# A causal softmax convolution and a cosine feed-forward layer on one core: weight conversion through PSUM scratch, row transposes from the third block on, and the last half block pair by pair

## The chip, the cores and the metric

The kernel runs on one core of a Trainium2 chip. The metric is device microseconds (us) of one execution. Before the change three runs gave 2300.47 us (median), 2298.91 and 2300.74. Engines are named as in the profile: PE (TensorE), PEld (its weight loads), DVE (VectorE), ACT (ScalarE), POOL (GpSimd), SP (the engine that issues all DMAs).

## The reference

```python
w = exp(weight_gen - max(weight_gen, -1)); w = w / (sum(w, -1) + 1e-9)   # (8, 4096, 8 heads, 7 taps)
x_pad = six zero rows ahead of x, along the sequence                      # x: (8, 4096, 192)
out[b, s, h, g] = sum over k of w[b, s, h, k] * x_pad[b, s + k, h, g]     # 8 heads of 24 columns
h = out.reshape(32768, 192) @ w_in                                        # w_in:  (192, 2048)
g = h * cos(h)
y = g @ w_out                                                             # w_out: (2048, 192)
```

The weights w_in and w_out arrive as 64-bit floats, everything else as 32-bit. The kernel splits each float operand of a product into a high part (fp32r) and a low part, and adds up the products of parts.

## The kernel before

**Blocks and periods.** Each of the 128 partitions holds 256 neighbouring rows of the sequence. A block is R = 4 of these rows on all partitions, 512 tokens; there are NB = 64 blocks. For each block POOL mixes the seven taps (`attention`: seven products, L239, and six additions, L256, in 128x768 tiles; its 13 steps are handed out two to four a period through `attentions`). PE turns the mixed block around (`transpose_all`, L292, into an `h` tile), and ACT and DVE split it (`split`, L282 and L284). The 2048 columns of h are taken in 8 pairs of 128-column chunks. A period i = 0..511 is one pair of one block: `ffn_in_first` and `ffn_in_second` (L322, L339) make h in PSUM; ACT rounds it to whole turns (L349), DVE takes the fraction (L353), ACT the sine (L357), DVE multiplies (L360), ACT makes the high part of g (L367) and DVE the low part (L371, called lo below). LAG = 6 periods later `ffn_out(j)` (L401) multiplies half a block of g, four pairs, by w_out, for two token rows at a time; `evacuate` copies the sums (L424, L428), and POOL adds the two halves (L441, L442). The last block does this on DVE.

**Two ways to transpose.** Blocks up to WHOLE = 6 go whole: in pair TR = 5 of the block before, eight PE transposes into an `h` tile, which ACT then copies out (L602). Later blocks go row by row (`transpose_row`, L301), into unused columns of the `acc` tile of `ffn_out`. They start at j = 8(b-2), that is at period 8b-10, whereas a whole transpose stands at period 8b-3. `until_mixed` makes sure that POOL's steps for the block have been issued ahead of it.

**PSUM.** `ps_h` has three tiles of 128x2x512 floats, `ps_m` one. An `h` tile is taken by the matmuls of a period and is free after its lo.

**Weights.** `two_parts` turns 64-bit words into 32-bit floats by integer operations: absolute value on ACT (L116), four DVE operations (L118, L121, L126, L130), casts on ACT (L132, L134), and the low part on POOL (L136). Its scratch `t1` lies in SBUF. Four pieces are converted before the first period or behind it, the other eleven in periods 1 to 9, by the table `late` (period of the conversion, loader, arguments), with their loads two periods ahead.

**Order.** Each engine executes in the order in which the Python code issues. SP carries the DMAs and, between them, small events (`traded`, L268) on which the second half of a period's matmuls waits. In period i the code issues for ACT and DVE: turns of i-1, high part of i-2, fraction of i-1, sine of i-1, conversion, lo of i-2, product of i-1; then the matmuls of i, loads, and the next steps of softmax and mixing. The prologue (L496 to L536) mixes block 0 on two engines, rows 0 to 2 on DVE and row 3 on POOL.

## Time and profile before

| | us |
|---|---|
| median of three runs | 2300.47 |
| the profiled execution | 2300.27 |
| its span, first to last instruction | 2298.4 |
| PE busy, of the span | 2215.7 (96%) |
| POOL busy | 2001.4 (87%) |
| DVE busy | 1935.6 (84%) |
| ACT busy | 1897.3 (83%) |
| first matmul of period 0 | 32.15 |
| first matmul of period 10 | 113.00 |
| last matmul ends, by its row | 2292.29 |

The rows in the prediction are of four kinds. The page's groups give a line, an engine, an operation, tiles and the count, then busy time and the mean ns of one. A row of the timeline gives the start in us, the duration, the engine and line, the tiles, the count of merged instructions, and in brackets the idle time before it with what ended it. A row of the windows gives for a stretch its length and each engine's busy time, then the granted PE clock, the DMA share and GB/s. A row of the chain gives start, length and the work merged into it.

### The profile page before, as it was taken

What the parts mean: (1) busy time and instruction counts of PE and PEld (TensorE: products, weight loads), DVE (VectorE), ACT (ScalarE), POOL (GpSimd) and SP (SyncE); (2) the same over time, 40 slices, a digit from 0 to 9 for tenths busy, and PEclk for the clock granted to TensorE, in tenths of its full rate; (3) what the DMA queues carried; (4) which work ended last, traced back from release to release, by engine and by line L of the source; (5) the groups of instructions that cost most, each with busy time, mean ns of one, the idle gap of its engine ahead of it and who ended that gap; (6) DMA issues with size and microseconds to landing.
All of it is one profiled execution on the core that took longest, in us unless ns stands there. A gap on an engine that the chain in (4) does not pass through costs nothing.

```text
span 2298.4 us, 60540 instructions
## 1 busy us (share of the span) xinstructions
PE 2215.7 (96%) x26472; PEld 2001.3 (87%) x26472; DVE 1935.6 (84%) x1664; ACT 1897.3 (83%) x2123; POOL 2001.4 (87%) x1445
## 2 busy tenths in 40 slices
PE   2699999999999999999999999999999999999998
PEld 1488888889899999998989888899998889999887
DVE  8988888888888888888888888888888888888886
ACT  2678888888888888888888888888888888888885
POOL 7679999899899989989899899989989899899940
PEclk9799999999999999999999999999999999999999
DMA  6112112112212112112212212212212212212100
GB/s 147 46 42 58 34 49 50 40 44 49 51 33 58 43 32 58 43 41 50 46 38 50 54 29 57 50 26 58 50 34 49 58 26 49 58 27 50 33 9 22
DMA packets 25767, 105.55 MB, mean 46 GB/s; under 512 B 2734, under 2 KB 6566, under 8 KB 25502
## 3 DMA queue, kind: packets, MB, share of 16 engines
q1 hardware_dynamic: 25502, 101.67, 18.5%
q8 instruction: 208, 3.41, 0.6%
q14 instruction: 57, 0.47, 0.1%
HBM read 76.50 MB, written 25.17 MB: 44 GB/s over the span
## 4 chain that ended last, share of the span: by engine, by line
PE 65%; POOL 19%; ACT 7%; DVE 6%; issue 3%; DMA 0%; SPq 0%; POOLq 0%; ACTq 0%
PE acc L401 31%; PE h L339 22%; PE h L322 11%; POOL xa L256 6%; POOL pr L239 6%; POOL part L441 2%; ACT part L424 2%; ACT turn L349 2%; POOL x_lo L284 1%; DVE glo L371 1%; ACT ghi L367 1%; POOL fin L442 1%; DVE turn L353 1%; ACT turn L357 1%; POOL taps L192 1%
## 5 line engine op out<-in xcount | busy, mean ns | idle before, releaser
L353 DVE TENSOR_TENSOR turn<-h,turn 128x1024 f32<-128x1024 f32 x512 | 625.7, 1222 | 277.4 <-ACT turn L349 277.4
L401 PE MATMUL acc<-wo,ghi 64*128 64x384 f32 x8144 | 815.4, 336 | 7.6 <-ACT part L428 3.9
L401 PEld LDWEIGHTS acc<-wo,ghi 64*128 64x128 f32 x8144 | 740.6, 185 | 49.1 <-ACT part L424 12.6
L256 POOL TENSOR_TENSOR xa<-xa,pr 128x768 f32<-128x768 f32 (+1 forms) x384 | 709.1, 1847 | 0.6
L357 ACT ACTIVATE turn<-turn 128x1024 f32<-128x1024 f32 x512 | 543.8, 1062 | 183.1 <-DVE turn L353 179.7
L360 DVE SCALAR_TENSOR_TENSOR h<-h,turn 128x1024 f32<-128x1024 f32 x512 | 631.0, 1232 | 49.4 <-ACT turn L357 49.3
L349 ACT ACTIVATE turn<-h 128x1024 int32<-128x1024 f32 x512 | 525.3, 1026 | 127.9 <-PE h L339 125.9
L371 DVE TENSOR_TENSOR glo<-h,ghi 128x1024 bf16<-128x1024 f32 x512 | 622.4, 1216 | 9.3 <-ACT ghi L367 9.3
L239 POOL TENSOR_TENSOR pr<-xt,taps 128x768 f32<-128x768 f32 (+1 forms) x384 | 592.2, 1543 | 12.2
L367 ACT CAST ghi<-h 128x1024 fp32r<-128x1024 f32 x512 | 518.1, 1012 | 17.8 <-DVE h L360 17.6
L401 PE MATMUL acc<-wo_b,glo 64*128 64x192 bf16 x8144 | 433.2, 243 | 0.0
L441 POOL TENSOR_TENSOR part<-part,part 128x768 f32<-128x768 f32 x126 | 233.0, 1850 | 174.5 <-ACT part L424 133.5
L401 PEld LDWEIGHTS <-glo 64*128 64x128 bf16 x8144 | 333.5, 94 | 27.6 <-issue 13.4
L339 PE MATMUL h<-x_lo,wa_hi 64*128 64x512 f32 x1024 | 252.4, 478 | 1.0
L322 PE MATMUL h<-x_lo,wa_hi 64*128 64x512 f32 x1024 | 216.8, 409 | 37.3 <-DVE glo L371 23.3
L424 ACT COPY part<-acc 128x1024 f32<-128x1024 f32 x228 | 227.0, 996 | 0.0
L339 PE MATMUL h<-x_lo,wb_hi 64*128 64x512 f32 x1024 | 210.7, 397 | 0.0
L339 PE MATMUL h<-x_hi,wa_hi 64*128 64x512 f32 x1024 | 210.6, 397 | 0.0
L322 PE MATMUL h<-x_hi,wa_lo 64*128 64x512 f32 x1024 | 209.1, 393 | 0.9 <-POOL wa_lo L136 0.8
L322 PE MATMUL h<-x_hi,wa_hi 64*128 64x512 f32 x1024 | 209.5, 394 | 0.0
L339 PE MATMUL h<-x_hi,wb_hi 64*128 64x512 f32 x1024 | 207.9, 391 | 0.0
L339 PE MATMUL h<-x_hi,wb_lo 64*128 64x512 f32 x1024 | 207.7, 391 | 0.0
(68 smaller groups left out, 2145.3 us busy)
## 6 DMA issues: line engine op xcount, KB each, us to landing
xt<-in_x_dram SPq DMA_DIRECT2D x62, 960.0 KB, 7.0
out_dram<-fin SPq DMA_DIRECT2D x63, 384.0 KB, 3.4
taps<-in_weight_gen_dram SPq DMA_DIRECT2D x15, 448.0 KB, 4.9
raw<-in_moe_w_out_dram SPq DMA_DIRECT2D x8, 384.0 KB, 3.4
raw<-in_moe_w_in_dram SPq DMA_DIRECT2D x10, 256.0 KB, 4.3
xt<-in_x_dram SPq DMA_DIRECT2D x1, 768.0 KB, 10.9
xt<-in_x_dram SPq DMA_DIRECT2D x1, 540.0 KB, 6.7
raw<-in_moe_w_in_dram SPq DMA_DIRECT2D x4, 128.0 KB, 5.8
```

The source lines that it names most:

```text
L239: eng.tensor_tensor(out=dst.rearrange("p r (h g) -> p r h g", h=H), in0=xt[:, k + ra:k + rb, :].rearrange("p r (h g) -> p r h g", h=H), in ...
L256: eng.tensor_tensor(out=xa[:, ra:rb], in0=xa[:, ra:rb], in1=old[:, ra:rb], op=ALU.add)
L322: nc.tensor.matmul(h[:, q, :], lhsT=w[rs, chunk(pair, q)], rhs=v[rs, q, :], start=(m == 0), stop=False, skip_group_check=True)
L339: nc.tensor.matmul(h[:, 1 - q, :], lhsT=w[rs, cs], rhs=v[rs, q ^ middle, :], start=False, stop=(m == len(prods) - 1), skip_group_check=True)
L349: nc.scalar.activation(out=t.bitcast(I32), in_=hs[i], func=AF.Identity, bias=0.25, scale=1.0)
L353: nc.vector.tensor_tensor(out=t, in0=hs[i], in1=t.bitcast(I32), op=ALU.subtract)
L357: nc.scalar.activation(out=t, in_=t, func=AF.Sin, bias=SIN_BIAS, scale=SIN_SCALE)
L360: nc.vector.scalar_tensor_tensor(out=hs[i], in0=hs[i], scalar=TWO_PI, in1=turns.pop(i), op0=ALU.mult, op1=ALU.mult)
L367: nc.scalar.copy(out=hi, in_=hs[i])
L371: nc.vector.tensor_tensor(out=lo, in0=hs.pop(i), in1=hi.bitcast(F32), op=ALU.subtract)
L401: nc.tensor.matmul(to, lhsT=g[rs, n, t * P:(t + 1) * P], rhs=w[rs, fc, :], start=(lo == 0 and c == 0 and (whole or s == 0)), stop=(lo == 1 ...
L441: eng.tensor_tensor(out=part, in0=part, in1=old, op=ALU.add)
```

## The change

- `two_parts` has a scratch of two halves handed to it by `make_room`: its sizes lie in an `h` tile of PSUM, only its last result in SBUF. The scale of the absolute value replaces one DVE operation, so three are left (L132, L136, L140 of the new file).
- In a period with a conversion the period's own `h` tile is taken first (`h_now`), then the scratch. Lo of i-2 now stands ahead of the conversion, the product of i-1 in its middle (after the casts of the conversion before, behind the sine).
- The prologue keeps block 0's sum for rows 0 to 2 and their taps in an `h` tile (`own`). Input rows are loaded ahead of weights, and the first weights are converted after the mixing. Three pieces of w_in (columns 0 to 255, a 512-wide piece for the `wb` table, columns 256 to 767) are converted there; before there were four.
- `late` gets a column for when to load; some loads use the tiles `part1` and `fin`, not yet needed then.
- WHOLE goes from 6 to 2: blocks 3 to 6 are transposed row by row. Mixing gets three steps a period up to period 11; the end of the softmax for blocks 3 to 6 moves from periods 10 to 12 to periods 6 to 8.
- The last four periods of `ffn_out` become `last_half`: all four token rows of the last half block, pair by pair, into two `h` tiles.

```diff
-    WHOLE = 6
+    WHOLE = 2
...
+    def make_room():
+        sizes = ps_h.tile([P, 2, CT], F32, name="h")
+        bits = work.tile([P, 2, CW], F32, name="t1", tag="turn", bufs=TMP)
+        room[:] = [(sizes[:, n, 0:CW].bitcast(I32), bits[:, n, :].bitcast(I32)) for n in range(2)]
...
-        t1 = work.tile([P, 2, CW], F32, name="t1", tag="turn", bufs=TMP)
-        size, bits = (shaped(t1.bitcast(I32)[:, k, 0:n])[..., 0] for k in range(2))
-        nc.scalar.activation(out=size.bitcast(F32), in_=top.bitcast(F32), func=AF.Abs)
+        size, bits = (shaped(t[:, 0:n], 1)[..., 0] for t in room.pop(0))
+        nc.scalar.activation(out=size.bitcast(F32), in_=top.bitcast(F32), func=AF.Abs, scale=F64_SCALE)
         yield
         nc.vector.tensor_scalar(
-            out=size.bitcast(F32), in0=size.bitcast(F32), scalar1=F64_SMALL, scalar2=None, op0=ALU.max)
-        yield
-        nc.vector.tensor_scalar(
-            out=size, in0=size, scalar1=0x07FFFFFF, scalar2=3,
-            op0=ALU.bitwise_and, op1=ALU.logical_shift_left)
+            out=size, in0=size, scalar1=3, scalar2=None, op0=ALU.logical_shift_left)
...
+    def last_half():
+
+        b = NB - 1
+        tiles = [ps_h.tile([P, 2, CT], F32, name="h") for _ in range(2)]
+        for p in range(HALF):
+            for lo in range(2):
+                g = g_parts[b * NPAIR + HALF + p][lo]
+                for t in range(R):
+                    acc = tiles[t // 2][:, t % 2, 0:(D if lo else 2 * D)]
+                    for n in range(2):
+                        fc = 2 * (HALF + p) + n
+                        nc.tensor.matmul(
+                            acc, lhsT=g[:, n, t * P:(t + 1) * P], rhs=(wo_b if lo else wo)[:, fc, :],
+                            start=(p == 0 and lo == 0 and n == 0),
+                            stop=(p == HALF - 1 and lo == 1 and n == 1), skip_group_check=True)
+        fin = work.tile([P, R, D], F32, name="fin")
+        for t in range(R):
+            old = sums.pop((b, t // 2))[:, t % 2] if t % 2 else sums[(b, t // 2)][:, 0]
+            part_ = work.tile([P, 2, CT], F32, name="part1", bufs=2)
+            part = part_[:, 0, 0:2 * D]
+            nc.vector.tensor_tensor(out=part, in0=tiles[t // 2][:, t % 2, 0:2 * D], in1=old, op=ALU.add)
+            (nc.vector if t == R - 1 else nc.gpsimd).tensor_tensor(
+                out=fin[:, t, :], in0=part[:, 0:D], in1=part[:, D:2 * D], op=ALU.add)
...
+    own = ps_h.tile([P, 2, CT], F32, name="h")
+    sm0 = softmax(0, R, nc.vector, to=own_taps)
     next(sm0)
-    b0 = w_in_b(0)
-    a0 = w_in_a(0, 256)
     load_rows(0)
     sm1 = softmax(R, 3 * R, nc.gpsimd)
     next(sm1)
-    a1 = w_in_a(256, 512)
-    b1 = w_in_b(1)
+    w_a0 = w_in_a(0, 256)
+    w_b0 = w_in_b(0)
     load_rows(1)
+    w_a1 = w_in_a(256, 768)
...
+        converts_now = converts.get(i, ())
+        h_now = None
+        if converts_now:
+            h_now = ps_h.tile([P, 2, CT], F32, name="h")
...
-        for c in converts.get(i - 1, ()):
-            next(c)
         if 0 <= i - 1 < N:
             dve_fraction(i - 1)
             act_cos(i - 1)
+        if 0 <= i - 2 < N:
+            dve_lo(i - 2)
+        if converts_now:
+            make_room()
+        for c in converts_now:
+            next(c)
+        all_of(*converts.pop(i - 1, ()))
         for c in now:
             next(c)
         splits.extend(later)
-        all_of(*converts.pop(i - 1, ()))
-        if 0 <= i - 2 < N:
-            dve_lo(i - 2)
         if 0 <= i - 1 < N:
             dve_g(i - 1)
+        for _ in range(3):
+            for c in converts_now:
+                next(c)
         all_of(*now)
```

How the instructions move is seen on two engines. First DVE, in a period that converts two pieces of w_out (`t` with a number is the SBUF scratch, `h` a PSUM tile, `raw` the loaded words). Before, from the fraction of period 1 on:

```order
L353 TENSOR_TENSOR turn<-h,turn 128x1024
L118 TENSOR_SCALAR t_307<-t_307 128x384
L118 TENSOR_SCALAR t_309<-t_309 128x384
L121 TENSOR_SCALAR t_307<-t_307 128x384
L121 TENSOR_SCALAR t_309<-t_309 128x384
L126 SCALAR_TENSOR_TENSOR t_307<-raw,t_307 128x384
L126 SCALAR_TENSOR_TENSOR t_309<-raw,t_309 128x384
L130 SCALAR_TENSOR_TENSOR t_307<-raw,t_307 128x384
L130 SCALAR_TENSOR_TENSOR t_309<-raw,t_309 128x384
L371 TENSOR_TENSOR glo<-h,ghi 128x1024
L360 SCALAR_TENSOR_TENSOR h<-h,turn 128x1024
```

And with the change, from the fraction of period 3 on:

```order
L369 TENSOR_TENSOR turn<-h,turn 128x1024
L387 TENSOR_TENSOR glo<-h,ghi 128x1024
L376 SCALAR_TENSOR_TENSOR h<-h,turn 128x1024
L132 TENSOR_SCALAR h<-h 128x384 x2
L136 SCALAR_TENSOR_TENSOR h<-raw,h 128x384 x2
L140 SCALAR_TENSOR_TENSOR t_402<-raw,h 128x384 x2
```

Lo and the product have moved ahead of the conversion, two of eight conversion operations are gone, and none of the six that are left has two inputs in SBUF. Of the three `h` tiles one is the scratch while such periods last; the order's waits show that period i's first matmul then waits for lo of period i-2, where it waited for lo of i-3.

Second PE, at the end of the program (`acc` is the tile of `ffn_out`, `ghi` with a number is the high part of one pair; rows of weight loads and of the low parts are left out). Before, the last two periods of `ffn_out` on their way over four pairs:

```order
L401 MATMUL acc_36022<-wo_81,ghi_35810 128x384 x2
L401 MATMUL acc_36022<-wo_81,ghi_35873 128x384 x2
L401 MATMUL acc_36022<-wo_81,ghi_35936 128x384 x2
L401 MATMUL acc_36022<-wo_81,ghi_35961 128x384 x2
...
L401 MATMUL acc_36022<-wo_81,ghi_35810 128x384 x2
L401 MATMUL acc_36022<-wo_81,ghi_35873 128x384 x2
L401 MATMUL acc_36022<-wo_81,ghi_35936 128x384 x2
L401 MATMUL acc_36022<-wo_81,ghi_35961 128x384 x2
```

With the change, the last half block:

```order
L481 MATMUL h_36023<-wo_81,ghi_35850 128x384 x4
L481 MATMUL h_36024<-wo_81,ghi_35850 128x384 x4
...
L481 MATMUL h_36023<-wo_81,ghi_35913 128x384 x4
L481 MATMUL h_36024<-wo_81,ghi_35913 128x384 x4
...
L481 MATMUL h_36023<-wo_81,ghi_35976 128x384 x4
L481 MATMUL h_36024<-wo_81,ghi_35976 128x384 x4
...
L481 MATMUL h_36023<-wo_81,ghi_36001 128x384 x4
L481 MATMUL h_36024<-wo_81,ghi_36001 128x384 x4
```

The last pair (ghi_36001) is now asked for in the last quarter of this work; before (ghi_35961), the first of the four periods already asked for all four pairs.

More of the change, by code (lines that the diff above doesn't have):

```diff
@@ L156, in tile_softmax_conv_then_cos_ffn, with w_out_2 @@
     w_out_v = w_out.rearrange("(c p) d -> p c d", p=P)
-    def w_out_2(q):
-        raw = words(2 * D)
+    def w_out_2(q, home="ghi"):
+        raw = words(2 * D, home)
         nc.sync.dma_start(out=raw.rearrange("p (c d) -> p c d", c=2),
@@ L175, in add_taps, with softmax @@
             old = out
-    def softmax(r0, r1, eng, early=True):
+    def softmax(r0, r1, eng, early=True, to=None):
         n = (r1 - r0) * H
@@ L227, in load_rows, with attention @@
             in_=x_v[:, :, (r0 - PAD + first) * D:(r0 + R) * D])
-    def attention(b, eng, ra=0, rb=R, spare=False):
+    def attention(b, eng, ra=0, rb=R, home="pr", t=None, acc=None):
         xt = rows[b]
-        t = taps[b]
+        if t is None:
+            t = taps[b][:, ra:rb]
         n = rb - ra
@@ L235, in attention @@
             mixed[b] = xa_
-        xa = mixed[b]
+        xa = mixed[b][:, ra:rb]
+        if acc is None:
+            acc = xa
         def product(k, dst):
@@ L248, in attention @@
             if k < K:
-                if spare:
-                    pr = work.tile([P, R, D], F32, name="pr", tag="turn", bufs=TMP)
-                else:
-                    pr = work.tile([P, R, D], F32, name="pr")
+                pr = work.tile([P, R, D], F32, name="pr", tag=home,
+                               bufs={"pr": 2, "turn": TMP, "part0": 3}[home])
                 product(k, pr[:, ra:rb])
@@ L255, in attention @@
             if old is not None:
[L256 to L257 removed]
+                eng.tensor_tensor(out=acc if k < K else xa, in0=acc, in1=old[:, ra:rb], op=ALU.add)
                 yield
@@ L503, in tile_softmax_conv_then_cos_ffn, with go_on @@
     next(sm1)
-    a1 = w_in_a(256, 512)
-    b1 = w_in_b(1)
+    w_a0 = w_in_a(0, 256)
+    w_b0 = w_in_b(0)
     load_rows(1)
+    w_a1 = w_in_a(256, 768)
     sm2 = softmax(3 * R, 3 * R + RW, nc.gpsimd)
     next(sm2)
-    load_weights(0)
-    load_weights(1)
-    for _ in range(3):
-        next(sm0)
-    next(b0)
-    next(a0)
-    all_of(sm0)
-    mix = attention(0, nc.gpsimd, 3, 4, spare=True)
-    for _ in range(3):
-        next(mix)
-    all_of(b0, a0)
-    next(mix)
-    for _ in range(3):
-        next(sm1)
-    next(a1)
-    next(b1)
-    all_of(mix, attention(0, nc.vector, 0, 3))
-    first = split(0, transpose_all(0), slice(0, CT), nc.vector)
-    next(sm2)
-    next(sm2)
-    all_of(sm1)
+    load_weights(-1)
+    def go_on(steps, n):
+        for _ in range(n):
+            next(steps, None)
+    all_of(sm0)
+    mix_v = attention(0, nc.vector, 0, RV, "part0", acc=own_acc,
+                      t=own_taps.rearrange("p (r h) k -> p r h k", h=H))
+    mix_p = attention(0, nc.gpsimd, RV, R, "turn")
+    go_on(mix_v, 6)
+    all_of(mix_p)
+    go_on(sm1, 2)
+    go_on(mix_v, 3)
+    go_on(sm1, 3)
+    go_on(mix_v, 1)
+    all_of(sm1)
+    bg = attentions()
+    go_on(bg, 1)
+    make_room()
+    go_on(w_a0, 1)
+    go_on(w_b0, 1)
+    all_of(mix_v)
+    tr = transpose_all(0)
+    go_on(w_a0, 3)
+    go_on(w_b0, 3)
+    first = split(0, tr, slice(0, CT), nc.vector)
+    go_on(first, 1)
+    all_of(w_a0, w_b0)
     all_of(first)
-    next(sm2)
+    go_on(sm2, 2)
+    make_room()
+    go_on(w_a1, 4)
+    go_on(sm2, 1)
     nc.scalar.activation(out=early, in_=early, func=AF.Sin)
-    bg = attentions()
-    for _ in range(4):
-        next(bg)
-    all_of(a1, b1)
+    all_of(w_a1)
+    go_on(bg, 4)
     N = NB * NPAIR
```

94 lines of the change are left out of this document (55 added, 39 removed).

## The prediction

> **What bounds the kernel now.** The windows come first; they tell the start from the rest (length, then PE, PEld, DVE, ACT, POOL busy, granted PE clock, DMA share, GB/s):
>
> ```profile
> 0.00:20.00 20.00, 0.00 (x0) 0.00 (x0) 11.66 (x21) 5.46 (x10) 11.04 (x20) 1.00 0.92 191
> 60.00:80.00 20.00, 12.82 (x54) 7.53 (x56) 17.56 (x22) 13.96 (x19) 13.68 (x10) 0.59 0.14 41
> 300.00:2100.00 1800.00, 1793.57 (x21842) 1640.49 (x21842) 1523.83 (x1287) 1542.69 (x1719) 1649.43 (x1193) 1.00 0.19 45
> ```
>
> From 300 to 2100 us PE is busy 1793.57 of 1800: PE sets the pace, and nothing in the change touches its matmuls there. At 60 to 80 us DVE is the fullest engine, and PE works at a low clock. So the change can win at the two ends only. How long they take is read from DVE's fraction (L353) in the timeline, which runs once a period: periods 0, 9, 16, 48 and 80.
>
> ```profile
> 42.36 1.22 DVE L353 TENSOR_TENSOR turn<-h,turn 128x1024 f32<-128x1024 f32 x1 [1.68 <-ACT turn L349]
> 114.34 1.22 DVE L353 TENSOR_TENSOR turn<-h,turn 128x1024 f32<-128x1024 f32 x1 [0.34 <-ACT turn L349]
> 147.92 1.23 DVE L353 TENSOR_TENSOR turn<-h,turn 128x1024 f32<-128x1024 f32 x1 [0.56 <-ACT turn L349]
> 292.60 1.23 DVE L353 TENSOR_TENSOR turn<-h,turn 128x1024 f32<-128x1024 f32 x1 [0.41 <-ACT turn L349]
> 429.75 1.23 DVE L353 TENSOR_TENSOR turn<-h,turn 128x1024 f32<-128x1024 f32 x1 [0.67 <-ACT turn L349]
> ```
>
> Periods 0 to 9 take 72.0 us, eight each. Blocks 2 to 5 (periods 16 to 47) take 144.7, the next four 137.15.
>
> Why DVE is slow at the start shows when one operation is set beside POOL's work:
>
> ```profile
> 46.24 1.61 POOL L239 TENSOR_TENSOR pr<-xt,taps 128x768 f32<-128x768 f32 x1
> 46.48 1.92 DVE L126 SCALAR_TENSOR_TENSOR t<-raw,t 128x512 int32<-128x512 int32 x1
> 64.83 0.69 DVE L126 SCALAR_TENSOR_TENSOR t<-raw,t 128x512 int32<-128x512 int32 x1
> 95.96 0.56 DVE L130 SCALAR_TENSOR_TENSOR t<-raw,t 128x384 int32<-128x384 int32 x1
> ```
>
> The same operation takes 1.92 us while POOL works (both inputs in SBUF, it ends just behind POOL's next start) and 0.69 alone. From 0.69 at 512 and 0.56 at 384 elements a 576-wide one should take 0.755, an estimate. The prices of a full period come from the page:
>
> ```profile
> L353 DVE TENSOR_TENSOR turn<-h,turn 128x1024 f32<-128x1024 f32 x512 | 625.7, 1222 | 277.4 <-ACT turn L349 277.4
> L256 POOL TENSOR_TENSOR xa<-xa,pr 128x768 f32<-128x768 f32 (+1 forms) x384 | 709.1, 1847 | 0.6
> L349 ACT ACTIVATE turn<-h 128x1024 int32<-128x1024 f32 x512 | 525.3, 1026 | 127.9 <-PE h L339 125.9
> L371 DVE TENSOR_TENSOR glo<-h,ghi 128x1024 bf16<-128x1024 f32 x512 | 622.4, 1216 | 9.3 <-ACT ghi L367 9.3
> L239 POOL TENSOR_TENSOR pr<-xt,taps 128x768 f32<-128x768 f32 (+1 forms) x384 | 592.2, 1543 | 12.2
> ```
>
> L353 and L371 take one input from PSUM and pay what an SBUF operation of 1024 would by the same slope (1.21). So I price operations on the PSUM scratch like unblocked SBUF ones, 0.69 at 512; the upper bound is the blocked 1.92, and no operation here goes from PSUM to PSUM with a constant.
>
> **The change part by part. 1, up to the first fraction.** The stage stands in these rows:
>
> ```profile
> 10.97 0.52 POOL L239 TENSOR_TENSOR xa<-xt,taps 128x192 f32<-128x192 f32 x1 [8.28 <-DMA xt<-in_x_dram]
> 22.61 1.03 DVE L239 TENSOR_TENSOR pr<-xt,taps 128x576 f32<-128x576 f32 x1
> 25.62 1.93 DVE L256 TENSOR_TENSOR xa<-xa,pr 128x576 f32<-128x576 f32 x2
> 27.70 1.94 PE L292 MATMUL h<-ident,xa 128*128 128x128 f32 x8 [27.70 <-DVE xa L256]
> 28.63 1.75 POOL L192 TENSOR_TENSOR taps<-taps,top 128x896 f32<-128x896 f32 x1 [2.48 <-DVE top L190]
> 31.54 1.28 ACT L532 ACT_TABLE_LOAD   x1
> 32.15 0.79 PE L322 MATMUL h<-x_lo,wa_hi 64*128 64x512 f32 x2 [2.51 <-DVE x_lo L284]
> 36.19 0.63 PE L339 MATMUL h<-x_hi,wb_hi 64*128 64x512 f32 x2
> ```
>
> The input rows reach the core at 10.97, behind 768 KB of weights; at the window's 191 GB/s these took 4.1 us, so loaded first they land at 6.9 (no gain at all would be 10.97). Mixing on DVE: 13 operations, 1.03 each beside POOL (22.61), 0.755 with sum and taps in PSUM: 9.8. Between them stand four small operations of the next softmax, 2.0 by their elements. They also wait: POOL's own 13 operations of 0.52 end at 13.7, its subtraction for that softmax at 14.6 (half of L192's 1.75), ACT's exponential at 15.2, and DVE is there at 14.3: 0.9. Block 0 is mixed at 19.6; before, at 27.55.
>
> Then a chain, with ACT's passes priced by L349 (1.03 for 1024 elements): transposes 1.94, high part 1.0, two casts (768 columns) 1.0, POOL's two low parts 2.0 (1.28 for 512, a row below), its subtraction L192 1.75, the exponential behind it 0.9, table load and first sine 1.5, the cast that period 1 needs 0.6, turns 1.03: 11.7. The six conversion operations on DVE (3.4), now between mixing and split, lie beside transposes and high part; were they blocked, 4 us more would show. The first fraction comes at 31.3, 11 us earlier.
>
> **2, periods 0 to 9.** With the scratch in one of three `h` tiles, period i's matmuls wait for lo of i-2. A converting period is then a chain: matmuls 4.67 at the low clock (32.15 to 36.82), turns 1.03, fraction 1.22, lo 1.21: 8.1. Behind lo, DVE has the product and the conversion (1.23 + 6 x 0.56 = 4.6), which fit beside matmuls and turns (5.7): DVE no longer sets the pace. From period 6 on, `ffn_out` adds its 2.1 us, but the clock is full:
>
> ```profile
> 2268.76 1.42 PE h L339 x12
> 2270.18 0.70 PE h L322 x6
> 2270.88 2.08 PE acc L401 x32
> 97.80 0.50 PE L322 MATMUL h<-x_lo,wa_hi 64*128 64x512 f32 x2 [3.25 <-DVE glo L371]
> 113.00 0.52 PE L322 MATMUL h<-x_lo,wa_hi 64*128 64x512 f32 x2 [3.96 <-DVE glo L371]
> 118.83 0.42 PE L322 MATMUL h<-x_lo,wa_hi 64*128 64x512 f32 x2
> ```
>
> 1.42 + 0.70 + 2.08 = 4.2 at full clock, plus the same 3.46: 7.7. But PE idles 3.46 us in each such period. At 113.00 an idle 3.96 cost 1.6 (5.83 instead of 4.2 until 118.83); at 97.80, 3.25 cost nothing. With three hand-overs between engines the idle time lies about halfway, so of the bounds 0 and 4.8 for periods 6 to 8 I charge two periods, 3.2. The Trainium skill (TensorE: Matmul & The Clock Gate, Part 1) says that the clock halves after an idle window of about 3.4 us that runs free. The rows agree, 3.25 and 3.96 lying on its two sides; by the rule as written all three periods fall, and the end is 1.6 later.
>
> Fraction to fraction: 5.6 (period 1's matmuls start early), 8.1, 9.3, 8.1, 7.7 (period 5 takes the tile that the scratch leaves and starts 0.4 sooner), 9.3 and 9.3 (7.7 + 1.6 for the clock), 7.7, 4.2; sum 69.3. The first 9.3, period 3, is a wait of 1.2 for a low part that POOL reaches late, behind six products (1.54) and four additions (1.85):
>
> ```profile
> 51.33 1.28 POOL L136 TENSOR_TENSOR wa_lo<-t,wa_hi 128x512 fp32r<-128x512 f32 x1 [1.28 <-ACT wa_hi L132]
> 138.78 2.83 POOL L256 TENSOR_TENSOR xa<-xa,pr 128x768 f32<-128x768 f32 x1
> 127.37 1.09 PE L292 MATMUL h<-ident,xa 128*128 128x128 f32 x8
> 133.05 0.40 PE L322 MATMUL h<-x_lo,wa_hi 64*128 64x512 f32 x2
> ```
>
> Fraction 9 then comes at 100.6, 13.7 earlier than 114.34. The moved DMAs: most late loads are issued earlier than before, into tiles free from the start; the last three w_out loads wait on SP for the conversion that empties their tile, and behind them stands the event of the next period, for which PE waits. Each of these conversions ends some 4 us ahead of that event, so nothing is charged; without that margin the whole period would slip.
>
> **3, periods 9 to 16.** All at PE's pace: 7 x 4.2, and 1.5 more for the whole transposes of block 2 (127.37 to 133.05 is 5.7). That is 31.0, before 33.6: fraction 16 at 131.6, 16.3 earlier. Here stands the change's own new demand: WHOLE = 2 wants block 3 at period 14, not 21. Its last low parts come with period 8 (fraction 7 at 88.7 plus sine, value and cast: 91); from there 1.0 and a softmax product 1.8, the block 7 x 1.54 + 6 x 1.85 = 21.9, one more low part 1.0, a pair of sums 2.9: mixed at 119.5. PE gets there at 120, behind period 14's high parts. A tie, so at no cost, with no slack. POOL regains it: 1649.43 of 1800 leaves 2.9 us a block.
>
> **4, blocks 2 to 5** lose four whole transposes with their copies; against later blocks that is 144.7 - 137.15 = 7.5. Part may be POOL's lateness: I take 7.
>
> **5, the end.**
>
> ```profile
> 2280.21 1.23 DVE L371 TENSOR_TENSOR glo<-h,ghi 128x1024 bf16<-128x1024 f32 x1 [1.08 <-ACT ghi L367]
> 2280.93 2.93 PE L401 MATMUL acc<-wo,ghi 128*128 128x384 f32 x8 [2.08 <-ACT part L428]
> 2287.83 1.68 PE L401 MATMUL acc<-wo,ghi 128*128 128x384 f32 x8 [0.94 <-ACT part L428]
> 2291.46 0.83 PE L401 MATMUL acc<-wo_b,glo 128*128 128x192 bf16 x8
> 2294.21 0.56 DVE L442 TENSOR_TENSOR fin<-part 128x384 f32<-128x384 f32 x1
> ```
>
> PE waits 2.1 and 0.9 us for copies that free the `acc` tile, and its first group runs at 2.93 instead of 1.68. From 2278.85 (2280.93 less 2.08) to 2292.29 it takes 13.4. Pair by pair, into two `h` tiles that are free by then, it needs the last pair only 6.3 us on, at 2285, when its lo (2281.44) is done. Four quarters of 2.15 (4.46 for the last two groups, halved, less latency) are 8.6. Behind PE stood a copy, an addition and a sum, 2.5 to the end of 2294.21's row; now four additions of 0.56 on DVE, the first two begun 0.3 before PE ends, and one short sum: 2.3. Gain 5.0.
>
> **Sum**: 16.3 + 7 + 5.0 = 28.3. The profiled execution took 2300.27 (span 2298.4 and 1.9 around it), 0.2 under the median, so 2300.27 - 28.3 = 2272.0, and 2272 beside the median.
>
> **The rivals.** *Mixing comes late.* POOL's tie at period 14 is lost; each late microsecond is PE's. An addition that met DVE's split took 2.83 (138.78) instead of 1.85; eight of the some fifty operations ahead of block 3 delayed so are 8 us: 2280. For it: no slack. Against: almost no DVE operation with two SBUF inputs is left beside them.
>
> *The scratch does not free DVE*, and POOL blocks half its operations, as before: a converting period becomes 3.7 + 3 x 0.56 + 3 x 1.92 = 11.1, 3.0 over 8.1, in four periods 12; the mixing gives back 13 x (1.03 - 0.755) = 3.6. 2288. Against: L353, with one input in PSUM, keeps 1222 ns over 512 runs beside a busy POOL.
>
> *Warm clock.* Periods 6 to 8 keep their clock and POOL is early: 3.2 and some of the front back, 2266.
>
> *POOL without a lead, slower than before.* With row transposes in every block POOL's sums wait for PE's copies and PE for POOL's blocks. Blocks 3 to 63 need only 0.47 us each to eat 28.3. At 35.0 a block instead of 34.3: 43 us, 2315. Against: 2.9 us spare per block, and from block 7 on the order is the old one.
>
> **How the numbers follow.** Forecast 0.62 (2272), late mixing 0.16, scratch 0.08, warm 0.10, slower 0.04. Its own errors (arrival of the rows, clock) are some 6 us either way. The range runs from 2262, below the warm case, to 2287, just short of the scratch case; what lies outside is most of that, the slower case and a tail below, under 0.2 together. A change under 0.2% (4.6 us) is about what a measurement cannot tell: faster 0.94, same 0.02, slower 0.04.
>
> **What would show it.** Fractions 0, 9, 16 at 31, 101, 132; conversions at 0.56 to 0.7 beside POOL; PE idle for 3.4 before periods 6 to 8; no POOL wait ahead of L317 at period 14; blocks 2 to 5 at 137; no PE wait behind the last L355. Wrong would be: a start above 36, POOL as the releaser of L317 in many blocks, or block times above 34.3 later on.

## The result and the profile after

The changed kernel takes 2276.1 us (median of four runs, 2275.44 to 2278.1) against 2300.46 for the kernel before in the same session (2298.91 to 2300.74): a ratio of 0.9897, with a 95% interval from 0.9885 to 0.9909. That is 24.4 us less; the prediction had 28.3 and 2272. The profiled execution has a span of 2276.3 us (2298.4 before), 22.1 less. It is the slowest of the four (2278.1), so the miss that its rows have to explain, 6.2, is larger than that of the medians, 4.1. The working below goes by these two spans.

The windows of the changed kernel (length, then PE, PEld, DVE, ACT, POOL busy, granted PE clock, DMA share, GB/s):

```profile
0.00:20.00 20.00, 0.00 (x0) 0.00 (x0) 13.47 (x24) 3.36 (x6) 12.24 (x25) 1.00 0.90 200
60.00:80.00 20.00, 14.31 (x88) 10.86 (x84) 16.65 (x22) 11.79 (x18) 19.75 (x15) 0.69 0.41 109
80.00:100.00 20.00, 12.54 (x100) 10.78 (x98) 11.19 (x13) 9.26 (x13) 9.53 (x8) 0.74 0.00 1
300.00:2100.00 1800.00, 1793.62 (x21844) 1655.78 (x21842) 1523.83 (x1287) 1542.78 (x1720) 1654.01 (x1196) 1.00 0.19 46
```

The middle of the run is what it was: 1793.62 busy PE us of 1800. From 60 to 80 us POOL is now the fullest engine, not DVE. From 80 to 100 no engine is full, PE works 12.5 of 20 us, and its clock is at 0.74: a stretch in which everybody waits in turn.

The fraction of each period again serves as the clock of the program (now L369; timeline of DVE; periods 0, 5, 6, 9, 16, 48 and 80):

```profile
31.66 1.23 DVE L369 TENSOR_TENSOR turn<-h,turn 128x1024 f32<-128x1024 f32 x1 [3.73 <-ACT turn L365]
70.62 1.23 DVE L369 TENSOR_TENSOR turn<-h,turn 128x1024 f32<-128x1024 f32 x1 [0.22 <-ACT turn L365]
81.59 1.23 DVE L369 TENSOR_TENSOR turn<-h,turn 128x1024 f32<-128x1024 f32 x1 [2.65 <-ACT turn L365]
106.70 1.23 DVE L369 TENSOR_TENSOR turn<-h,turn 128x1024 f32<-128x1024 f32 x1 [1.21 <-ACT turn L365]
138.16 1.22 DVE L369 TENSOR_TENSOR turn<-h,turn 128x1024 f32<-128x1024 f32 x1 [0.43 <-ACT turn L365]
275.32 1.23 DVE L369 TENSOR_TENSOR turn<-h,turn 128x1024 f32<-128x1024 f32 x1 [0.66 <-ACT turn L365]
412.44 1.23 DVE L369 TENSOR_TENSOR turn<-h,turn 128x1024 f32<-128x1024 f32 x1 [0.66 <-ACT turn L365]
```

Against the rows of before that makes a budget, all in us of the two profiled executions:

| stretch | predicted | measured |
|---|---|---|
| up to fraction 0 | 31.3 | 31.66 |
| fractions 0 to 5 (5.6 + 8.1 + 9.3 + 8.1 + 7.7) | 38.8 | 38.96 |
| fractions 5 to 9 (9.3 + 9.3 + 7.7 + 4.2) | 30.5 | 36.08 |
| fractions 9 to 16 | 31.0 | 31.46 |
| blocks 2 to 5, gain | 7 | 7.5 |
| behind fraction 511, gain (22.86 before, 18.04 now) | 5.0 | 4.8 |

One line is off, by 5.6 us, and 5.0 of these lie in periods 6 to 8 (31.3 for 26.3). PE's timeline there (first matmuls of periods 6, 7 and 8 with the idle time ahead of them, and the high products of `ffn_out`):

```profile
73.12 0.79 PE L338 MATMUL h<-x_lo,wa_hi 64*128 64x512 f32 x2 [3.64 <-DVE glo L387]
74.53 2.79 PE L417 MATMUL acc<-wo,ghi 64*128 64x384 f32 x16
...
84.10 0.80 PE L338 MATMUL h<-x_lo,wa_hi 64*128 64x512 f32 x2 [3.73 <-DVE glo L387]
85.51 2.79 PE L417 MATMUL acc<-wo,ghi 64*128 64x384 f32 x16
...
94.72 0.50 PE L338 MATMUL h<-x_lo,wa_hi 64*128 64x512 f32 x2 [3.73 <-DVE glo L387]
95.49 2.19 PE L417 MATMUL acc<-wo,ghi 64*128 64x384 f32 x16
```

PE waits for DVE's low part 3.64 to 3.73 us ahead of each, as foreseen, and in all three the clock is then low: 16 products take 2.79 us at the low clock and 1.58 at the full one (in period 9), and in period 8 the clock falls in the middle of them. From the first matmul to the last these periods take 7.2, 6.9 and 5.9 us. The prediction had 4.2 at the full clock, and 1.6 more in two of the three.

### The profile page after: what moved, and what is told of

The parts are those of the page before. It is cut to its first block, busy times and chain, and to the rows that moved or that the text cites. A ratio compares the mean times of both kernels' runs of the same rounds, so it can differ in the third digit from the quotient of the medians.

```text
span 2276.3 us, 60636 instructions
## 1 busy us (share of the span) xinstructions
PE 2212.3 (97%) x26504; PEld 2017.7 (89%) x26504; DVE 1904.1 (84%) x1647; ACT 1896.8 (83%) x2129; POOL 2003.6 (88%) x1464
## 3 DMA queue, kind: packets, MB, share of 16 engines
q8 instruction: 208, 3.41, 0.6%
## 4 chain that ended last, share of the span: by engine, by line
PE 68%; POOL 19%; ACT 7%; issue 3%; DVE 3%; DMA 0%; POOLq 0%; SPq 0%; ACTq 0%; DVEq 0%
PE acc L417 32%; PE h L355 23%; PE h L338 12%; POOL xa L272 6%; POOL pr L257 5%; POOL part L456 2%; ACT turn L365 2%; ACT part L440 2%; POOL x_lo L299 1%; ACT ghi L383 1%; POOL fin L457 1%; DVE turn L369 1%; ACT turn L373 1%; POOL taps L202 1%; DVE glo L387 1%
## 5 line engine op out<-in xcount | busy, mean ns | idle before, releaser
L369 DVE TENSOR_TENSOR turn<-h,turn 128x1024 f32<-128x1024 f32 x512 | 625.8, 1222 | 295.5 <-ACT turn L365 295.3
L417 PEld LDWEIGHTS <-glo 64*128 64x128 bf16 x8112 | 334.9, 94 | 22.2 <-issue 10.7
L440 ACT COPY part<-acc 128x1024 f32<-128x1024 f32 x244 | 243.1, 996 | 0.0
L338 PE MATMUL h<-x_hi,wa_lo 64*128 64x512 f32 x1024 | 210.8, 393 | 1.5 <-POOL wa_lo L146 1.5
L355 PE MATMUL h<-x_hi,wa_lo 64*128 64x512 f32 x1024 | 209.3, 392 | 0.0
```

Of the source, the lines that this page charges most:

```text
L338: nc.tensor.matmul(h[:, q, :], lhsT=w[rs, chunk(pair, q)], rhs=v[rs, q, :], start=(m == 0), stop=False, skip_group_check=True)
L355: nc.tensor.matmul(h[:, 1 - q, :], lhsT=w[rs, cs], rhs=v[rs, q ^ middle, :], start=False, stop=(m == len(prods) - 1), skip_group_check=True)
L369: nc.vector.tensor_tensor(out=t, in0=hs[i], in1=t.bitcast(I32), op=ALU.subtract)
L417: nc.tensor.matmul(to, lhsT=g[rs, n, t * P:(t + 1) * P], rhs=w[rs, fc, :], start=(lo == 0 and c == 0 and (whole or s == 0)), stop=(lo == 1 ...
L440: nc.scalar.copy(out=part, in_=acc)
```

## The experiments

Each kernel is the changed one with the edit shown; times are medians, and each kernel was run beside the kernel before (2300.4 to 2301.3 in all sessions). "Of the changed kernel" means against its 2276.1.

### PE kept busy ahead of periods 6, 7 and 8

Eighteen transposes of the identity, into unused columns of `acc`; nobody reads them.

```diff
+    def keep_busy(i, n):
+        j = i - LAG
+        open_ = accs.get(j // 2) if j >= 0 else None
+        spare = open_
+        if open_ is None:
+            spare = ps_m.tile([P, 2, CT], F32, name="acc")
+        for k in range(n):
+            nc.tensor.matmul(spare[:, k % 2, 2 * D:CT], lhsT=ident, rhs=ident, is_transpose=True,
+                             start=(open_ is None and k < 2), stop=True, skip_group_check=True)
...
             if j >= 0:
                 evacuate(j)
+            if 5 <= i <= 7:
+                keep_busy(i, 18)
```

> The changed kernel, with 18 transposes of the identity, whose result nobody reads, behind the last matmul of periods 5, 6 and 7, so that PE does not idle before periods 6, 7 and 8. In the changed kernel's profile PE idles 3.64, 3.73 and 3.73 us there, the granted clock falls to 0.50 at 72.3, 82.6 and 96.3 and comes back at 79.1, 89.4 and 99.6, and the matmuls of these periods take 7.2, 6.9 and 5.9 us instead of 4.2. Theory (the clock is the whole miss, and each fall costs half the low stretch that has matmuls in it: 3.0 + 2.7 + 1.7 = 7.4): granted clock 1.00 throughout periods 6 to 8, steps between fractions of 7.7 to 8.0, fraction 9 at about 99.5 instead of 106.7, and 2276.1 - 7.4 = 2268.7. First rival (only a part is the clock, as the prediction priced it, 1.6 a fall, and the rest are late engines): 2271 to 2273, with another engine as the releaser. Second rival (POOL takes it back: block 3 is not mixed earlier, and PE waits about 7 for it at period 14): no change, 2276.

Measured: 2271.72 (2270.94 to 2272.51), 4.4 less than the changed kernel. PE's timeline of this run (first matmuls and high products of periods 6 and 7):

```profile
72.33 0.50 PE L338 MATMUL h<-x_lo,wa_hi 64*128 64x512 f32 x2 [1.53 <-DVE glo L387]
73.10 1.60 PE L417 MATMUL acc<-wo,ghi 64*128 64x384 f32 x16
...
80.91 0.50 PE L338 MATMUL h<-x_lo,wa_hi 64*128 64x512 f32 x2 [1.99 <-DVE glo L387]
81.81 2.77 PE L417 MATMUL acc<-wo,ghi 64*128 64x384 f32 x16
```

Two windows of its PE (length, busy, granted clock, DMA share, GB/s):

```profile
78.11:81.52 3.41, 1.42 (x14) 1.00 0.00 0
81.52:84.93 3.41, 3.41 (x28) 0.51 0.02 5
```

Period 6 goes at the full clock now (1.60), period 8 too, but in period 7 the clock still fell, at 81.5, although PE had been idle for only 1.99 us. So two of three falls are gone; fractions 5 to 9 take 31.15 instead of 36.08. The total lies in the range of the first rival, but not for its reason: each wait still ends with DVE's low part, as before, and the steps behind the two periods that kept the clock are shorter by 2.3 and 1.7, the third by 1.0. POOL took nothing back: PE waited 0.16 for it at period 14, as in the changed kernel (0.17). The clock is the larger part of the miss, but the filling was too short for a whole cure, and the 7.4 was not reached.

### Half the filling: what makes the clock fall

```diff
-                keep_busy(i, 18)
+                keep_busy(i, 9)
```

> As the first run of fillings, but with 9 transposes of the identity (1.1 us) behind periods 5, 6 and 7 instead of 18, so that some 2.5 of PE's idle 3.6 us stay before periods 6, 7 and 8. Theory (what counts is PE's busy share in fixed windows of 3.41 us: windows of 1.45 and less lost the clock in the runs so far, those of 1.54 to 1.61 kept it): a window that holds the 2.5 idle us whole has 0.9 busy and falls, one in which the boundary cuts them does not: one or two falls of 1.7 to 3 us, none of them with an idle time of 3.4, total 2272 to 2274.5. Rival (the clock falls only after a stretch of about 3.4 us without a matmul): no fall in periods 6 to 8, total 2268.5 to 2270.

Measured: 2274.28 (2272.73 to 2275.28). PE idles 2.52, 2.51 and 2.51 us ahead of periods 6, 7 and 8. In this trace every change of the clock lies a multiple of 3.41 us from the others, so I cut PE's time at these points (window, length, busy, granted clock, DMA share, GB/s):

```profile
68.85:72.26 3.41, 1.55 (x13) 1.00 0.45 124
79.09:82.50 3.41, 2.26 (x19) 1.00 0.00 0
82.50:85.91 3.41, 2.05 (x22) 1.00 0.02 5
89.33:92.74 3.41, 0.90 (x8) 1.00 0.00 0
```

After the first and the last of these windows the clock fell (at 72.3 and 92.8), after the middle two it stayed. The same idle time of 2.5 lies whole in the last window and is cut in two by the boundary at 82.50. That decides for the share of a window, and against the need for 3.4 us without a matmul. The same cut through the changed kernel:

```profile
68.93:72.35 3.42, 0.55 (x6) 1.00 0.60 153
79.17:82.58 3.41, 1.19 (x10) 1.00 0.00 0
89.41:92.83 3.42, 1.58 (x16) 1.00 0.00 0
92.83:96.24 3.41, 1.52 (x16) 1.00 0.00 0
96.24:99.65 3.41, 3.41 (x31) 0.50 0.00 0
```

It fell after 0.55, 1.19 and 1.52, not after 1.58. The edge is near half a window and not sharper than that in these traces, where the ends of matmuls are modelled: over all fourteen traces every window with up to 1.52 busy us lost the clock and none with 1.72 or more, while between 1.54 and 1.71 eight windows kept it and eight lost it. A low clock then lasts until a window is nearly full (2.89 and 3.16 busy us raised it, 2.87 and 3.08 did not). In periods 6 to 8 that was one window or two, and a fall cost 1.7 to 3.0 us there.

### Filling behind periods 0 to 7

```diff
-            if 5 <= i <= 7:
+            if i <= 7:
```

> The changed kernel, with the 18 transposes of the identity behind the last matmul of every period from 0 to 7, not only of 5 to 7. Theory (a full clock lets periods 1 to 5 go at 5.8 instead of 8.1, until POOL, busy without a gap from 30.7 to 82.2, sets the pace, with at most 2.6 to win): the 2271.7 of the run with three fillings less 1 to 2.6: 2269 to 2270.7. First rival (POOL does not bound these periods): 2263 to 2268. Second rival (at the low clock the 18 transposes take 4.4, more than the idle 3.7, so they delay PE and the clock never rises): 2274 to 2278.

Measured: 2269.46 (2269.23 to 2271.22), 6.6 less than the changed kernel. Beside the cure of all three falls (fractions 5 to 9 take 30.3; in period 6 DVE's softmax operations hold the fraction back by 1.2) only 1 us came out of periods 1 to 5, as the theory with POOL as the bound said. What held them shows in the next experiments.

### The scratch in SBUF

The size of a word is worked out in the SBUF tile that takes its bits; the third `h` tile stays with PE.

```diff
-        sizes = ps_h.tile([P, 2, CT], F32, name="h")
...
-        room[:] = [(sizes[:, n, 0:CW].bitcast(I32), bits[:, n, :].bitcast(I32)) for n in range(2)]
+        room[:] = [(bits[:, n, :].bitcast(I32),) * 2 for n in range(2)]
```

> The changed kernel, with the conversions' scratch in SBUF only (a word's size is worked out in the tile that takes its bits), so the third h tile stays with PE and no conversion reads PSUM. Theory (PSUM is what frees DVE; by the prediction's rival half of the operations beside POOL are blocked, 1.92 instead of 0.56): 3 operations more by 1.36 for each of four periods with two pieces, so steps between fractions 1 to 5 of 9 to 11 instead of 8.3, 9.5, 8.2, 7.1, and a mean of the conversion operations of 512 and 384 elements above 1.0 in periods 1 to 5. In periods 6 to 8 the third tile ends the wait for lo, so they take 5.5 to 7 instead of 10.5, which is worth 9 to 12; the total 2274 to 2283. Rival (blocking is no longer a matter, the tile is all that counts): conversions at 0.56 to 0.69, steps of 5.7 to 7.5 in periods 1 to 5, total 2262 to 2268.

Measured: 2294.1 (2293.73 to 2295.78), 18.0 more, worse than either theory's end. The conversion operations on DVE in the changed kernel (groups by form, 31 to 110 us: busy us, mean ns):

```profile
L136 DVE SCALAR_TENSOR_TENSOR h<-raw,h 128x384 int32<-128x384 int32 x8 | 4.5, 562 | 0.3
L140 DVE SCALAR_TENSOR_TENSOR t<-raw,h 128x384 int32<-128x384 int32 x8 | 4.3, 550 | 0.2
```

and with the scratch in SBUF (31 to 120 us):

```profile
L140 DVE SCALAR_TENSOR_TENSOR t<-raw,t 128x384 int32<-128x384 int32 x8 | 14.4, 1805 | 0.1
L136 DVE SCALAR_TENSOR_TENSOR t<-raw,t 128x384 int32<-128x384 int32 x8 | 13.1, 1645 | 0.1
```

The same work takes three times as long beside POOL's mixing when both inputs lie in SBUF. Over all forms the conversions take 53.8 us of DVE instead of 20.8. Steps between fractions 1 to 5 are 14.8, 10.8, 10.7 and 11.5 (the prediction's rival had 11.1); periods 6 to 8 give 3.6 back with the third tile (fractions 5 to 9 take 32.48). Fraction 16 comes at 154.11, later than in the kernel before (147.92), so the PSUM scratch is what this change of the start lives on. The Trainium skill (GPSIMD Engine Reference, Specifications) says that POOL shares its SBUF interfaces with DVE and that DVE operations with two SBUF inputs contend with it. These rows agree and give the price, 0.56 against 1.65 to 1.81 us.

### A tile for the scratch that PE does not need

In periods 1 to 5 the scratch lies in the `acc` tile, which `ffn_out` first uses in period 6. PE then has all three `h` tiles.

```diff
-    def make_room():
-        sizes = ps_h.tile([P, 2, CT], F32, name="h")
+    def make_room(pool=ps_h, name="h"):
+        sizes = pool.tile([P, 2, CT], F32, name=name)
...
-            make_room()
+            make_room(*(ps_m, "acc") if i < LAG else ())
```

> The changed kernel; the scratch of the conversions in periods 1 to 5 lies in the acc tile, which no matmul uses before period 6, so PE has three h tiles in these periods and no longer waits for the low part of two periods ago. Theory (the chain matmuls, turns, fraction, low part sets these periods, as the prediction's second part has it): with the chain gone DVE's own work sets them, 3.66 and the conversions at the changed kernel's 0.69 and 0.56: 5.7, 7.4, 7.4, 7.0, 6.6 for steps that took 8.3, 9.5, 8.2, 7.1 and (to fraction 6, with the clock) 11.0: fraction 5 about 5 earlier, total 2270 to 2273, and PE waits for DVE's low part gone before period 6. Rival (POOL sets them: it is busy without a gap from 30.7 to 82.2 in the changed kernel, 2.6 idle after that): the waits turn into waits for low parts of POOL (L146), fraction 6 at most 2.6 earlier, total 2273.5 to 2276.

Measured: 2273.33 (2273.11 to 2274.09), 2.8 less. Without the chain the four steps from fraction 1 on are 7.27, 10.47, 6.81 and 6.44, in the changed kernel 8.26, 9.48, 8.24 and 7.14. (The expectation set DVE's sums one step late: its 5.7 belongs to the step from fraction 0, which takes 5.62, and 7.4, 7.4, 7.0 and 6.6 to these four.) Three steps went as the chain theory says, and one, the 10.47, the rival's way; the total lies between the two ranges. In PE's timeline of this run, period 3:

```profile
49.80 0.80 PE L338 MATMUL h<-x_hi,wa_lo 64*128 64x512 f32 x2 [8.12 <-POOL wa_lo L146]
```

and in POOL's, what it waits for:

```profile
48.48 1.27 POOL L146 TENSOR_TENSOR wa_lo<-t,wa_hi 128x512 fp32r<-128x512 f32 x1
```

However early PE comes to period 3, it gets no further before 49.8 (49.85 in the changed kernel, 49.95 with filling everywhere): the low part that it needs stands on POOL behind ten steps of block 1's mixing.

### POOL's order changed

```diff
-        for _ in range(3 if i < 12 or i < 64 and i % 4 == 0 else 2):
+        for _ in range((1, 1, 5, 5)[i] if i < 4 else 3 if i < 12 or i < 64 and i % 4 == 0 else 2):
```

This comes on top of the scratch in `acc`.

> The run with the scratch of periods 1 to 5 in the acc tile (2273.3), with POOL's mixing of block 1 thinned to one step in periods 0 and 1 and made up for by five in periods 2 and 3, so that four operations fewer (6.8 us) stand on POOL ahead of the first low part of w_in's columns 768 to 1280. There PE waited 8.12 us before period 3, until 49.8, as in the changed kernel (49.85). Theory (the order on POOL, not its load, holds period 3): that low part starts at 42 to 43, the wait is gone, the step from fraction 2 to 3 is DVE's 7.4 instead of 10.5, and the total 3 less, 2270.3 give or take the 1.4 of the clock's phase. Rival (POOL's load holds it: it has no gap from 30.7 to 82, so what goes behind comes back as a wait for block 1 at period 5 or for a later low part): less than 1 us, 2272.5 to 2274.

Measured: 2272.14 (2270.71 to 2272.49), 1.2 less than without it, between the two theories. PE's waits for POOL in this run:

```profile
42.76 0.79 PE L338 MATMUL h<-x_hi,wa_lo 64*128 64x512 f32 x2 [1.35 <-POOL wa_lo L146]
52.58 0.51 PE L355 MATMUL h<-x_hi,wb_lo 64*128 64x512 f32 x2 [3.84 <-POOL wb_lo L146]
55.33 1.97 PE L308 MATMUL h<-ident,xa 128*128 128x128 f32 x8 [1.39 <-POOL xa L272]
```

The wait of 8.12 has shrunk to 1.35, and the step from fraction 2 to 3 is 7.20, as the order theory said: fraction 4 is 3.6 earlier. But then PE waits for a later low part and for block 1, as the load theory said: at fraction 5 only 1.8 of it is left. Behind that the clock, low from 52.9 to 73.4 and from 80.2 to 83.6, decides the rest. POOL's order held period 3; a step further POOL's load does.

### Combinations

The first has filling behind periods 0 to 7, POOL's new order, and the last three softmax steps a period earlier:

```diff
-        if step in SOFTMAX and step != EXP or NPAIR - 2 <= i < NPAIR + 1:
+        if step in SOFTMAX and step != EXP or NPAIR - 3 <= i < NPAIR:
```

> The run with the identity transposes behind periods 0 to 7 (2269.5), with the same thinning of POOL's steps, and the last three steps of the softmax of blocks 3 to 6 a period earlier (so that block 3's mixing stands ahead of the last low part but one). In that run PE still waited 1.57 for the low part of POOL before period 3's second pair of matmuls, and the clock fell from 49.8 to 56.6. Theory: the wait goes, the clock stays up in period 3, 2 to 4 less: 2265.5 to 2267.5, and L317 of period 14 does not wait for POOL. Rival (POOL's load): block 1 or block 3 is late instead, PE waits over 1 us for POOL at period 5 or 14, 2268.5 to 2270.

Measured: 2272.81 (2270.32 to 2274.16), 3.3 more than with the old order, and no theory foresaw that. The profiled execution is the fastest of the four (2270.32). It shows the step from fraction 2 to 3 shortened from 9.87 to 7.21, one fall of the clock at 70.6 that the old order did not have, and 1.0 lost at period 15 to a wait for DVE (shown below). What the slower three lost, no trace shows; it stays open.

The second has the scratch in `acc`, POOL's order as it was, and 26 transposes behind periods 6 and 7:

```diff
+            if 6 <= i <= 7:
+                keep_busy(i, 26)
```

> The scratch of periods 1 to 5 in the acc tile, and 26 transposes of the identity (3.2 us at full clock) behind the last matmul of periods 6 and 7, so that no more than 0.5 us of PE's idle time is left there. Theory (both gains add: 5 from the chain, and 4.4 to 6 from the clock): 2265 to 2268, granted clock 1.00 from period 6 on. Rival (POOL bounds the first, so 2.6 at most remain of it): 2268 to 2271. Second rival (with periods 6 to 8 faster POOL is late with block 3, and PE waits for it at period 14): L317 waits over 2 us for POOL there.

Measured: 2270.89 (2270.19 to 2271.67). The falls ahead of periods 7 and 8 are gone, but the clock was low from 62.0 to 75.6, through all of period 6, which had no filling ahead of it: the step to fraction 6 takes 10.42, and the gains add only in part, since the wait of 7.83 for POOL in period 3 stands here too. The total is what the first rival gave.

The third puts everything together:

```diff
+            if 5 <= i <= 7:
+                keep_busy(i, (16 if i == 5 else 24))
```

> Everything together: scratch of periods 1 to 5 in the acc tile, POOL's steps thinned, the softmax steps a period earlier, and 16, 24 and 24 identity transposes behind periods 5, 6 and 7. Theory (the parts add): 2270.3 of the run without the fillings, less 3 to 5 of the clock: 2265 to 2267. Rival (the transposes behind period 5 must wait for the conversions to leave the acc tile and delay period 6, and the clock, low from period 3 on, makes them longer than the wait that they fill): 2268 to 2271.

Measured: 2268.88 (2268.72 to 2268.98), ratio 0.9864 to the kernel before (95% interval 0.9847 to 0.988), and 7.2 us less than the changed kernel: the best of all. From 65.7 to the last matmuls of the program the clock stays up, fractions 5 to 9 take 29.1, and its four runs lie within 0.3 us, those of the changed kernel within 2.7. It ended 1.9 above the theory's range and in the rival's, though period 6 was not delayed as the rival had it: the step to fraction 6 takes 8.17. One microsecond is lost at period 15 again, where PE waits 1.07 for DVE. What holds DVE up is the low part of the split, with two SBUF inputs. In this run it began 0.1 us behind the start of one of POOL's products (118.15, 1.54) and ended 1.1 behind that product's end; in the changed kernel it met only the last 0.5 of POOL's operation. First this run, then the changed kernel:

```profile
118.26 2.51 DVE L299 TENSOR_TENSOR x_lo<-part,x_hi 128x1024 fp32r<-128x1024 f32 x1
...
128.50 1.55 DVE L299 TENSOR_TENSOR x_lo<-part,x_hi 128x1024 fp32r<-128x1024 f32 x1
```

### The parts of the change undone one by one

Block 0's rows loaded behind the first weights, as before:

```diff
-    load_rows(0)
-    sm1 = softmax(R, 3 * R, nc.gpsimd)
-    next(sm1)
-    w_a0 = w_in_a(0, 256)
-    w_b0 = w_in_b(0)
+    w_b0 = w_in_b(0)
+    w_a0 = w_in_a(0, 256)
+    load_rows(0)
+    sm1 = softmax(R, 3 * R, nc.gpsimd)
+    next(sm1)
```

> The changed kernel, with block 0's input rows loaded behind the 768 KB of first weights, as before the change. Theory (the prediction's first step: the rows' arrival sets the mixing, 4.1 us for the weights): rows at 11, first fraction at 35.5 to 35.8 instead of 31.66, and the whole 4 later, 2280. Rival (the softmax of block 0 or the chain of casts behind the mixing sets the front, and the rows have slack): first fraction under 33, total 2276 to 2277.5.

Measured: 2281.0 (2280.63 to 2281.62), 4.9 more. DVE's first product of the mixing, in this run:

```profile
10.70 0.76 DVE L257 TENSOR_TENSOR h<-xt,h 128x576 f32<-128x576 f32 x1 [4.59 <-DMA xt<-in_x_dram]
```

and in the changed kernel:

```profile
7.28 0.76 DVE L257 TENSOR_TENSOR h<-xt,h 128x576 f32<-128x576 f32 x1 [1.13 <-DMA xt<-in_x_dram]
```

It starts 3.4 later, and the first fraction comes 3.4 later too (35.09): the rows' arrival has no slack in the changed kernel. In the profiled executions 2.5 of it is left at the end, because the clock's falls lie otherwise; the medians say 4.9.

WHOLE = 6 again:

```diff
-    WHOLE = 2
+    WHOLE = 6
```

> The changed kernel with WHOLE = 6: blocks 3 to 6 are transposed whole again, as before the change. Theory (the prediction's fourth part): blocks 2 to 5 take 144.7 instead of 137.2, and nothing else moves, 2276.1 + 7.5 = 2283.6. Rival (part of these 7.5 us is POOL's lateness, which row transposes only move: the need for block 3 at period 14 instead of 21 costs PE something): less than 5 between fractions 16 and 48, or blocks 6 to 9 shorter, 2278 to 2281.

Measured: 2283.07 (2282.01 to 2284.0), 7.0 more. Fractions 16 to 48 take 143.6 instead of 137.2, and from block 6 on each block takes what it did. That is 6.45 of the 7.5. The last 1.1 of what blocks 2 to 5 lost in the kernel before is not due to WHOLE: it lies in block 2 alone (36.60 before, 35.41 in this run), where PE waited 1.11 for DVE. The split's low part began there 1.4 us ahead of the end of an addition of POOL and ended 1.1 behind it. Before:

```profile
174.03 2.47 DVE L284 TENSOR_TENSOR x_lo<-part,x_hi 128x1024 fp32r<-128x1024 f32 x1
178.92 0.50 PE L322 MATMUL h<-x_lo,wa_hi 64*128 64x512 f32 x2 [1.11 <-DVE glo L371]
```

and in this run, where it met only the last 0.2 of POOL's operation and PE does not wait:

```profile
163.70 1.28 DVE L299 TENSOR_TENSOR x_lo<-part,x_hi 128x1024 fp32r<-128x1024 f32 x1
```

The last half block in row groups, in the `acc` tile, as before:

```diff
-                if j == N - HALF:
-                    last_half()
-                return
+                if j >= N:
+                    return
+                ffn_out(j)
```

with the sums on DVE and the store of two rows each put back in `evacuate`.

> The changed kernel, with the last half block done as before the change (row groups in the one acc tile, copies, sums of two rows on DVE). Theory (the end is worth what the spans show behind the last fraction, 22.1 - 17.3 = 4.8): 2276.1 + 4.8 = 2280.9, PE waits of about 2.1 and 0.9 for copies behind the last second part of ffn_in. Rival (the earlier parts of the end would have hidden most of it, since block 63's first half now starts in another phase): less than 2 us, 2276 to 2278.

Measured: 2279.99 (2278.73 to 2281.84), 3.9 more; in the traces 3.3 more behind fraction 511 (21.35 against 18.04). The end of this run:

```profile
2262.44 1.67 PE L417 MATMUL acc<-wo,ghi 128*128 128x384 f32 x8 [2.07 <-ACT part L444]
2267.84 1.67 PE L417 MATMUL acc<-wo,ghi 128*128 128x384 f32 x8 [0.94 <-ACT part L444]
...
2274.21 0.56 DVE L458 TENSOR_TENSOR fin<-part 128x384 f32<-128x384 f32 x1
```

and of the changed kernel:

```profile
2261.34 1.66 PE L481 MATMUL h<-wo,ghi 128*128 128x384 f32 x8
2267.68 1.66 PE L481 MATMUL h<-wo,ghi 128*128 128x384 f32 x8
...
2272.18 0.36 DVE L491 TENSOR_TENSOR fin<-part 128x192 f32<-128x192 f32 x1
```

The two waits for copies are what they were before the change, but the group behind the first takes 1.67 here and took 2.93 there. The profiled execution of before had lost its clock in that wait (its window there, from 2277.41, had 1.44 busy us; in this run, from 2258.42, 1.94). The 1.5 between 4.8 and 3.3 is that fall (1.26 here, 0.29 in the low products behind), not the work's order.

## Why the prediction was right or wrong

**Faster, and by the parts named: right.** Of its six stretches five lie within 0.5 us. The rival of a scratch that frees nothing fell with the conversions' 0.55 and 0.56 beside POOL. Its price, 16 us, was near what the scratch in SBUF then cost, 18, but partly by luck: it had half of the operations held up, nearly all were, and periods 6 to 8 gave 3.6 back. The prediction also says that no operation goes from PSUM to PSUM with a constant; L132 does (`h` to `h`, a shift by 3), and took 0.56 like the others. The rival of late mixing fell with one row of PE's timeline at period 14:

```profile
126.14 0.28 PE L317 MATMUL acc<-ident,xa 64*128 64x64 f32 x2 [0.17 <-POOL xa L272]
```

The tie held at 0.17, also where PE came 5.7 earlier, since POOL's last steps of the conversions wait for ACT (in the changed kernel 2.57, 7.83 and 1.90 us ahead of L146 at 84.82, 95.45 and 104.71) and come earlier with it. PE and POOL were both some 6 us later than the prediction had them. POOL without a lead did not happen either: block times from block 6 on are unchanged.

**Step 1, the front: right.** Rows at 7.3 (6.9 predicted; the weights ahead of them cost 3.4, not 4.1), mixing operations of 0.74 to 0.77 (0.755), first fraction 0.4 late. The experiment with the rows behind the weights shows that the arrival counts one for one, as the step took it.

**Step 2, periods 0 to 5: right in its sum and in its mechanism.** The chain through the low part of two periods ago set these periods; with a third tile for PE the steps fell toward DVE's own work. The wait for POOL at period 3 was 0.92 (1.2 predicted). What the prediction did not see is how hard POOL's order holds that period: PE can come 7 us earlier and starts at the same time.

**Step 2, periods 6 to 9: the waits right, the price of the clock wrong, and this is nearly the whole miss, 5.6 of 6.2.** The failed term is "of the bounds 0 and 4.8 for periods 6 to 8 I charge two periods, 3.2". All three periods lost the clock. Without a fall fractions 5 to 9 take 29.1 (the combined kernel) or 30.3 (filling behind periods 0 to 7, with DVE's softmax still in period 6), with all three 36.1: the falls cost 5.8 to 7.0, more than even the upper bound of 4.8. Two readings were wrong. The first took the idle time of 3.46 as halfway between 3.25, which had cost nothing, and 3.96, which had cost 1.6. In these traces the length of the idle time does not decide; the busy share of a fixed window does, and with it the phase. The same windows in the kernel before, around the wait of 3.25 (the first two), around that of 3.96, and behind it:

```profile
92.88:96.29 3.41, 1.68 (x18) 1.00 0.20 41
96.29:99.71 3.42, 1.91 (x20) 1.00 0.00 0
...
109.95:113.36 3.41, 0.35 (x4) 1.00 0.00 0
113.36:116.77 3.41, 3.41 (x24) 0.50 0.02 5
```

The 3.25 was cut by a boundary, and half a window of work stood on either side; the 3.96 left 0.35. The second: the price of 1.6 came from this one fall, which a full window followed at once; where PE's work begins inside a window, that window is not full, the low clock lasts into the next, and a fall costs up to 3.0. The Trainium skill (TensorE: Matmul & The Clock Gate, Part 1) says that the clock halves after an idle window of about 3.4 us and that the window runs free. The changes of the clock, all on a raster of 3.41 us, agree with the window; that it must be idle is not what the runs show, since 1.42 busy us of 3.41 were not enough to keep the clock. The prediction read that rule as three falls, which came 1.6 nearer to the result, but taken by its words an idle time of 3.46 would seldom hold a whole window of 3.41, so being nearer was luck.

By the 29.1, the remaining 1.8 of the 5.6 is no clock: a period without a fall takes 8.0 to 8.2, not 7.7 (PE's wait is 3.6 to 3.7, not 3.46, and the first matmul behind it 0.5), and the step from fraction 8 to 9 takes 4.8 in every run of the new order, not 4.2.

**Step 3: right** (31.46 for 31.0). **Step 4: right in size**, with 6.45 of 7.5 shown as the whole transposes' own. **Step 5: right in size**, but 1.5 of its 4.8 rested on the 2.93 row, a fall of the clock in the one execution that was profiled.

## What to carry to other kernels

Where PE waits a few microseconds in each of several periods, price the clock by cutting its time into the windows that the clock's own changes mark, and count a fall for each window under about half busy; a few matmuls that nobody reads, put into the wait, cost nothing there and took 4.4 us back at once. When an operation on DVE must run beside a busy POOL, an input in PSUM can be worth much more than a new order (here 18 us against 1.2 for POOL's new order), but count whose buffer the scratch takes: here it was PE's third tile, while another lay unused. And when an engine is in time for a low part that another issues in a fixed order, look at the place in that order first: starting PE 7 us earlier gained nothing at that point here.
